# A two-layer decode block on one Trainium2 core: eight more units of K kept on the chip, a ring of 12 units, one narrow wo a layer, transposes for the gathers, and a last product in column fourths

## The chip, the core and the metric

The kernel runs on one core of one Trainium2 chip. The metric is device time in microseconds (us) of one execution; the time before the change is the median of three runs. The core has a matrix engine (PE, with its weight loads shown apart as PEld), a vector engine (DVE), a scalar engine (ACT), GpSimd (POOL) and a sync engine (SP), which here issues nearly all loads. Loads from the main memory (HBM) into the on-chip memory (SBUF) are carried by 16 DMA engines. PE writes to PSUM, which has eight banks of 128 partitions x 512 floats.

## The reference

Two equal layers, with the same weights and the same K and V caches. Two sequences (B = 2), one new token each, model width 512. Attention has 32 query heads of 128 and 8 KV heads; each KV head serves four query heads over 32768 cached positions. All is float32.

```python
def _A_ref(x, k_cache, v_cache, wq, wo):       # attention
    q = (x @ wq).reshape(B, Sq, Hq, Dh).transpose(0, 2, 1, 3)
    k, v = jnp.repeat(k_cache, rep, axis=1), jnp.repeat(v_cache, rep, axis=1)
    scores = jnp.einsum("bhqd,bhkd->bhqk", q, k) * (Dh ** -0.5)
    o = jnp.einsum("bhqk,bhkd->bhqd", _softmax(scores), v)
    return o.transpose(0, 2, 1, 3).reshape(B, Sq, Hq * Dh) @ wo
def _B_ref(x, w_gate, w_up, w_down):           # feedforward, 1792 wide
    return (_gelu(x @ w_gate) * (x @ w_up)) @ w_down

x = A_x
for layer in range(2):                          # the same weights and caches in both
    x = x + _A_ref(_layernorm(x), A_k_cache, A_v_cache, A_wq, A_wo)
    x = x + _B_ref(_layernorm(x), B_w_gate, B_w_up, B_w_down)
```

The two caches together have 2 x 268 MB. They don't fit on the chip, so each layer reads them anew.

## The kernel before

**Units and places.** SBUF is one array M of 110 units; a unit is 128 partitions x 512 floats, 256 KB. Three big slots A, B and C have 32 units each (0, 32 and 64 on), a zone from unit 96 has the rest; units 106 to 109 hold scratch. All loads stand in one list (`plan`), written out by hand in the order in which they are issued. `pump` (L105) issues the head of the list on SP as soon as its units are marked free, and never passes it; `free` (L120) marks units free where the program text has used them. So SP waits, in order, for the use of what stood in a place before.

**Attention.** A pair is one KV head g and one sequence b, 16 pairs a layer; layer 0 goes through them upward, layer 1 downward. K and V of a pair come in two halves each: four chunks (k0, k1, v0, v1) of 32 units, 8 MB, which pass through the three slots in turn. `scores` (L287) multiplies a 32-column window that holds the four queries with each unit of K (L282), into four column groups of a bank, and takes the maximum (`peak`). `softmax` (L299) exchanges the maxima, takes the exponentials on ACT and transposes them on PE (L310). `values` (L318) multiplies them with V (L326) into one bank. `combine` (L333) copies that bank to SBUF (L335), sums its pieces on PE with four products against a selection matrix (L337), and multiplies with the reciprocal sum (L339). After both sequences of a KV head, `project` (L341) multiplies by that head's part of wo, four units, into the bank W, where the residual x has been put beforehand (`restart`, L233).

**Center.** `center` (L238) copies W to SBUF with a row sum on ACT, and brings x and x minus its mean into columns on PE: eight instructions against a constant of four columns (L242) and a product of the row sums with -1/512 (L243); two copies take the results to xw (L245) and xin (L246). `deviation` makes 1/sqrt(variance).

**Feedforward.** `feedforward` (L348): the gate and up weights, 28 units (`gu`), are multiplied with xw (L363), first 16 units, then 12; `gelu` on ACT and DVE; `hidden` transposes the result (L392); `down` multiplies with the 14 units of `wd` (L407) into W. In layer 1 the last unit of wd goes another way: W is copied to SBUF (L422), the unit itself is the stationary operand of four products (L427), W's four groups are added with a selection matrix (L430), and a copy (L433) and a DMA (L434) give the output, 128 x 8 floats.

**The layer boundary.** The last pair of layer 0 is also the first of layer 1. Its v stays on the chip (64 units), of k1 the first 24 units stay (`KC1`), and of k0 five units are copied to PSUM banks (L466, L471): 93 units kept. The rest of the memory, 20 units, is a ring of five places of four units (`PL`, `RING`): through it come gu and wd of layer 0, wq of layer 1 (its last four units, `wq7`, first), then the eight missing units of k1 (L183 and L184). k0's other 27 units are loaded again (L185). The loop at L500 multiplies the seven query pieces and, after each, scores some of the k1 units that are kept, which frees their places for k0.

## Time and profile before

| what | value |
|---|---|
| median of three runs | 2578.67 us (2578.1 to 2579.88) |
| the profiled execution, its own time | 2578.3 us |
| span in it, first to last instruction | 2576.5 us |
| HBM read | 1105.03 MB, 429 GB/s over the span |
| PE busy; weight loads; DVE; ACT | 1373.9; 406.2; 130.8; 80.9 us |
| mean granted PE clock | 0.733 of full speed |
| instructions | 20195, of them 9430 matmuls and as many weight loads |

The profile is a page on one execution, taken by the hardware profiler, and answers that can be asked of its trace. A row of a group of instructions has the line, the engine and the operation, the tiles (written <- read), shapes and count, then the busy time, the mean of one in ns, and the engine's idle time before them with what ended it. `L326 PE` is line 326 on the matrix engine. A timeline row begins with the start and the duration in us, and ends with the idle time and its releaser in brackets. A row of the windows view begins with a stretch of time and has the busy time of each engine (with the count of instructions), the granted clock, the mean busy share of the 16 DMA engines, and GB/s. A row of DMA issues has the size and the median time from issue to landing. "SPq L114" is a DMA issue by SP. A float32 product is issued as two instructions, so four units are "x8"; a transpose is one.

### The profile page before, as it was taken

Reading aid. Unit: us, or ns where it says so; the run is one execution under the profiler, and the core shown is the slowest. Engines: PE = TensorE matmul, PEld = TensorE weight load, DVE = VectorE, ACT = ScalarE, POOL = GpSimd, SP = SyncE. Lnnn points to the kernel's source line nnn. Section 1 sums busy time; section 2 is a strip of 40 time slices with the busy share of each in tenths; the row PEclk is TensorE's granted clock in tenths of the full one; section 3 lists DMA queues with packets and bytes.
Section 4 is the critical chain, followed back from the end, with each engine's and each line's share of the span. In section 5 each row is a group of like instructions: output and inputs, shape, how many; then the busy total and the mean of one; then the engine's idle time right before and its main releaser. Section 6 shows DMA issues by size and latency. Waiting matters only on the chain.

```text
span 2576.5 us, 20195 instructions
## 1 busy us (share of the span) xinstructions
PE 1373.9 (53%) x9430; PEld 406.2 (16%) x9430; DVE 130.8 (5%) x390; ACT 80.9 (3%) x195; POOL 3.8 (0%) x12
## 2 busy tenths in 40 slices
PE   3554545455545544555576555454455544554556
PEld 1111111111111111111122111111111111111112
DVE  0000000000000000000010000000000000000001
ACT  0000000000000000000010000000000000000000
POOL 0000000000000000000000000000000000000000
PEclk9777777777766777777788677777767777776778
DMA  9999999999999999999999999999999999999998
GB/s 424 433 429 435 431 433 435 431 437 429 433 433 428 436 437 428 434 432 433 423 403 439 432 429 436 430 433 436 432 431 435 431 434 432 434 431 431 436 435 347
DMA packets 27587, 1106.33 MB, mean 429 GB/s; under 512 B 3312, under 2 KB 3440, under 8 KB 4208
## 3 DMA queue, kind: packets, MB, share of 16 engines
q1 hardware_dynamic: 27216, 1104.95, 99.5%
q8 instruction: 74, 1.21, 0.2%
q10 hardware_dynamic: 288, 0.09, 0.0%
q14 instruction: 9, 0.07, 0.0%
HBM read 1105.03 MB, written 0.00 MB: 429 GB/s over the span
## 4 chain that ended last, share of the span: by engine, by line
DMA 62%; PE 25%; another core or an unknown queue 12%; issue 0%; ACT 0%; DVE 0%; SPq 0%; DVEq 0%; ACTq 0%
DMA M<-in_vt 52%; PE bank L326 16%; DMA M<-in_kt 8%; PE bank L282 7%; DMA M<-in_wd 1%; PE bank L345 1%; PE bank L337 1%; DMA M<-in_gu 0%; DMA M<-in_wq 0%; ACT M L335 0%; PE bank L407 0%; PE bank L258 0%; PE bank L310 0%; DVE oT L339 0%
## 5 line engine op out<-in xcount | busy, mean ns | idle before, releaser
L282 PE MATMUL bank<-M,qw 128*32 128x512 f32 x4096 | 591.6, 741 | 544.9 <-DMA M<-in_kt 544.9
L326 PE MATMUL bank<-M 128*16 128x512 f32 x4096 | 580.3, 730 | 513.9 <-DMA M<-in_vt 513.9
L282 PEld LDWEIGHTS bank<-M,qw 128*32 128x32 f32 x4096 | 143.5, 133 | 981.0 <-DMA M<-in_kt 578.9
L326 PEld LDWEIGHTS bank<-M 128*16 128x16 f32 x4096 | 137.1, 112 | 930.4 <-issue 915.6
L285 DVE TENSOR_REDUCE sm<-bank 128x1 f32<-128x512 f32 x64 | 44.2, 691 | 1125.4 <-PE bank L282 1125.4
L307 ACT ACTIVATE M<-bank,sm 128x512 f32<-128x512 f32 x64 | 43.4, 683 | 1239.1 <-DVE sm L302 1239.1
L310 PE MATMUL bank<-cst,M 128*128 128x128 f32 x256 | 51.1, 348 | 42.2 <-ACT M L307 42.0
L339 DVE TENSOR_TENSOR oT<-bank,sm 128x4 f32<-128x4 f32 x32 | 5.2, 162 | 1138.8 <-PE bank L337 1138.8
L335 ACT COPY M<-bank 128x512 f32<-128x512 f32 x32 | 18.8, 586 | 1141.0 <-PE bank L326 1141.0
L311 DVE COPY M<-bank 128x512 f32<-128x512 f32 x64 | 43.8, 691 | 60.8 <-PE bank L310 60.8
L337 PE MATMUL bank<-cst,M 128*128 128x4 f32 x256 | 34.1, 256 | 22.5 <-ACT M L335 22.5
L310 PEld LDWEIGHTS bank<-cst,M 128*128 128x128 f32 x256 | 37.0, 176 | 52.5 <-ACT M L307 52.5
L337 PEld LDWEIGHTS bank<-cst,M 128*128 128x128 f32 x256 | 31.3, 192 | 52.0 <-ACT M L335 52.0
L301 PE MATMUL bank<-cst,sm 128*128 128x128 f32 x32 | 10.3, 323 | 35.1 <-DVE sm L300 35.1
L345 PE MATMUL bank<-M,oT 128*2 128x512 f32 x128 | 22.0, 765 | 4.1 <-DVE oT L339 4.1
L363 PE MATMUL bank<-M,xw 128*32 128x512 f32 x112 | 21.4, 737 | 4.6 <-DVE M L387 2.6
L315 PEld LDWEIGHTS bank<-cst,sm 128*128 128x128 f32 x128 | 23.1, 253 | 0.0
L315 PE MATMUL bank<-cst,sm 128*128 128x4 f32 x128 | 21.1, 270 | 0.0
L258 PE MATMUL bank<-M,xw 128*32 128x512 f32 x128 | 19.0, 706 | 2.1 <-DMA M<-in_wq 1.4
L235 PE MATMUL bank<-cst,xin 128*2 128x128 f32 x40 | 6.0, 301 | 23.3 <-DMA cst<-in_consts 23.3
L301 PEld LDWEIGHTS bank<-cst,sm 128*128 128x128 f32 x32 | 4.3, 133 | 64.1 <-DVE sm L300 64.1
L307 ACT ACTIVATION_READ_ACCUMULATOR M<-bank,sm 128x1 f32 x64 | 12.5, 196 | 0.0
(68 smaller groups left out, 128.5 us busy)
## 6 DMA issues: line engine op xcount, KB each, us to landing
M<-in_wo SPq DMA_DIRECT2D x16, 1024.0 KB, 51.1
M<-in_vt SPq DMA_DIRECT2D x6, 2048.0 KB, 43.0
M<-in_kt SPq DMA_DIRECT2D x3, 4096.0 KB, 18.0
M<-in_kt SPq DMA_DIRECT2D x5, 2048.0 KB, 15.5
M<-in_wq SPq DMA_DIRECT2D x2, 4096.0 KB, 17.0
M<-in_gu SPq DMA_DIRECT2D x8, 1024.0 KB, 23.4
M<-in_wq SPq DMA_DIRECT2D x8, 1024.0 KB, 9.3
M<-in_gu SPq DMA_DIRECT2D x3, 2048.0 KB, 33.2
```

The costliest lines, as they stand in the source:

```text
L258: nc.tensor.matmul(Q[32 * k:32 * k + 32, :], xw[:, k, XO - 2 * g:XO - 2 * g + 32], mem(u), start=start, stop=stop)
L282: nc.tensor.matmul(S[32 * t:32 * t + 32, :], w[:, 28 - 4 * c:60 - 4 * c], mem(u), start=start, stop=stop)
L285: nc.vector.tensor_reduce(mx[:, h:h + 1], S, axis=AX.X, op=OP.max)
L307: nc.scalar.activation(p[h], S[h], AF.Exp, bias=bias, scale=SCALE, accum_out=ls[:, h:h + 1])
L310: nc.tensor.transpose(S[h][:, k * P:(k + 1) * P], p[h][:, k * P:(k + 1) * P], ident)
L311: nc.vector.tensor_copy(mem(U_PT + h), S[h])
L315: nc.tensor.matmul(X[:, P:P + REP], ls[:, h:h + 1].to_broadcast([P, P]), mask, start=(h == 0), stop=(h == 1))
L326: nc.tensor.matmul(acc[32 * t:32 * t + 16, :], mem(U_PT + h)[:, k * P + 32 * t + 16 * e:k * P + 32 * t + 16 * e + 16], mem(u), start=(h == ...
L335: nc.scalar.copy(md, acc)
L337: nc.tensor.matmul(X[:, :REP], md[:, c * P:(c + 1) * P], sel[:, 4 * c:4 * c + 4], start=(c == 2), stop=(c == 1))
L345: nc.tensor.matmul(W[32 * t:32 * t + NB, :], oT[:, t, :], mem(u + t), start=(t > 0 and first), stop=final)
L363: nc.tensor.matmul(G[v][32 * t:32 * t + 32, :], xw[:, k, XO:XO + 32], mem(un), start=(k == 0), stop=(k == KC - 1))
```

## The change

- `KC1` goes: all 32 units of k1 stay, with 64 of v and five of k0 in PSUM, 101 units. The two loads of k1 go.
- The ring has three places of four units (`PL`). wq of layer 1 comes in pieces of 4 and 2 units, with places written out; `kseq` is the order in which k1 is scored, and the five units in PSUM are copied to places of k1 (`held`).
- `NARROW`: for KV head 6 in layer 0 and 1 in layer 1, query heads 2 and 3 of wo are loaded as before (two units), and heads 0 and 1 come as `wn`: the same 512 KB as 16 partitions x 16 units, written in the list after the last chunk of that KV head, into the slot whose turn it is. `project` multiplies them in 16 products of 16 rows, after it has brought oT into that form with eight small products and a copy. The slots of layer 1 follow from where layer 0 ends (`roles`).
- `combine` scales the copied bank with the reciprocal sum (`linvc`, made in `softmax`), transposes its four parts on PE and sums the pieces on DVE. `center` does likewise, and adds the mean's product on DVE.
- In layer 1's `down`, each unit of wd is multiplied in four parts of 128 columns, each into a column group of its own; `restart(split=True)` puts x there likewise. The output is the bank's first 128 columns as a whole, 128 x 128 floats, and the host picks rows from it.

```diff
@@ -33,18 +33,21 @@
-PL = [96, 100, 104, 88, 92]
+PL = [96, 100, 104]
-RING = [2, 3, 4, 0, 1]
-KC1 = 24
+RING = [2, 0, 1]
+NARROW = [6, 1]
+NH = 2
+NG = P // 16
+NC = NH * NG
...
@@ -111,7 +112,10 @@
-            nc.sync.dma_start(mem(u, n), src)
+            if key[0] == "wn":
+                nc.sync.dma_start(M[:16, u * U:(u + n) * U], src.rearrange("(e r) n -> e r n", r=4))
+            else:
+                nc.sync.dma_start(mem(u, n), src)
...
@@ -162,35 +166,49 @@
-            places.append(PL[RING[at % 5]])
+            places.append(PL[RING[at % 3]])
...
     def add_wo(l, g):
-        add(("wo", l, g), wo[g], PL[g % 2], 4)
+        if g == NARROW[l]:
+            add(("wo", l, g), cols(wo[g], NH, REP - NH), PL[g % 2], REP - NH)
+        else:
+            add(("wo", l, g), wo[g], PL[g % 2], REP)
+
+    def sequence(pairs, l):
+        todo = []
+        for n, (g, b) in enumerate(pairs):
+            todo += [(g, b, nm_, h) for nm_ in "kv" for h in range(2)]
+            if g == NARROW[l] and (n + 1 == len(pairs) or pairs[n + 1][0] != g):
+                todo.append((g, b, "w", 0))
+        return todo
     for l in range(2):
         if l == 0:
             stream("wq", 0, wq, 32, (16, 16), (SLOT_A, SLOT_A + 16))
             ring = [SLOT_B, SLOT_C, SLOT_A]
-            todo = [(g, b, nm_, h) for g, b in orders[0] for nm_ in "kv" for h in range(2)]
+            todo = sequence(orders[0], 0)
+            roles = [ring[(len(todo) - 4 + i) % 3] for i in range(3)]
         else:
-            ring = [SLOT_A, SLOT_B, SLOT_C]
+            last0, last1, lastv = roles
+            ring = [lastv, last0, last1]
             g, b = orders[1][0]
-            add(("wq7",), cols(wq, 28, 4), PL[RING[1]], 4)
-            ring_stream("wq", 1, wq, 28, 2)
-            add(("k1", 0), cols(kt[b, g, 1], KC1, 4), PL[1], 4)
-            add(("k1", 1), cols(kt[b, g, 1], KC1 + 4, 4), PL[2], 4)
-            stream("k0", 1, kt[b, g, 0], KFREE, (8, 8, 8, 3), [SLOT_C, SLOT_C + 8, SLOT_C + 16, PL[3]])
+            add(("wq7",), cols(wq, 28, 4), ZONE + 2, 4)
+            stream("wq", 1, wq, 28, (4, 2, 2, 4, 4, 2, 2, 4, 4), [ZONE + i for i in (6, 10, 0, 2, 6, 10, 0, 2, 6)])
+            stream("k0", 1, kt[b, g, 0], KFREE, (8, 8, 8, 3), [last1 + i for i in (0, 8, 16, 24)])
             g, b = orders[1][1]
-            chunk("k", 1, g, b, 0, SLOT_C, (8, 8, 16))
-            chunk("k", 1, g, b, 1, SLOT_A, (16, 16))
-            chunk("v", 1, g, b, 0, SLOT_B)
+            chunk("k", 1, g, b, 0, last1, (8, 8, 16))
+            chunk("k", 1, g, b, 1, lastv, (16, 16))
+            chunk("v", 1, g, b, 0, last0)
             add_wo(1, g)
-            chunk("v", 1, g, b, 1, SLOT_C)
-            todo = [(g, b, nm_, h) for g, b in orders[1][2:] for nm_ in "kv" for h in range(2)]
+            chunk("v", 1, g, b, 1, last1)
+            todo = sequence(orders[1][2:], 1)
         for i, (g, b, nm_, h) in enumerate(todo):
+            if nm_ == "w":
+                add(("wn", l, g), wn[l], ring[i % 3], NC)
+                continue
             last = i == len(todo) - 1
             second = (g, b) == orders[l][orders[l].index((g, b))] and orders[l].index((g, b)) % 2 == 1
             if nm_ == "v" and h == 1 and second and not last:
@@ -202,8 +220,8 @@
             ring_stream("gu", 0, gu, 28, 0)
             ring_stream("wd", 0, wd, 14, 7)
         else:
-            stream("gu", 1, gu, 28, (8, 8, 8, 4), [SLOT_C + 8 * i for i in range(4)])
-            stream("wd", 1, wd, 14, (4, 4, 2, 2, 1, 1), [SLOT_A + i for i in (0, 4, 8, 10, 12, 13)])
+            stream("gu", 1, gu, 28, (8, 8, 8, 4), [ring[(len(todo) - 3) % 3] + 8 * i for i in range(4)])
+            stream("wd", 1, wd, 14, (4, 4, 2, 2, 1, 1), [ring[(len(todo) - 2) % 3] + i for i in (0, 4, 8, 10, 12, 13)])
...
@@ -230,7 +247,11 @@
-    def restart(alone=False):
+    def restart(alone=False, split=False):
+        if split:
+            for c in range(KC):
+                nc.tensor.matmul(W[32 * c:32 * c + NB, :P], xin[:, c, :], ident, start=True, stop=False)
+            return
         for c in range(KC):
             nc.tensor.matmul(W[0:NB, c * P:(c + 1) * P], xin[:, c, :], ident, start=(c == 0),
                              stop=alone and c == KC - 1)
@@ -238,12 +259,11 @@
     def center():
         ws = mem(U_PT + 1)
         nc.scalar.activation(ws, W, AF.Copy, accum_out=rs)
-        for c in (2, 3, 0, 1):
-            nc.tensor.matmul(X[:, c * 4:(c + 1) * 4], ws[:, c * P:(c + 1) * P], two, start=(c == 2), stop=False)
-        nc.tensor.matmul(X[:, :KC * 4], rs.to_broadcast([P, P]), neg, start=False, stop=True)
-        xc = X[:, :KC * 4].rearrange("p (c w b) -> p c w b", w=2, b=NB)
-        nc.vector.tensor_copy(xw[:, :, XO:XO + NB], xc[:, :, 1, :])
-        nc.scalar.copy(xin, xc[:, :, 0, :])
+        for c in range(KC):
+            nc.tensor.transpose(X[:, c * P:(c + 1) * P], ws[:, c * P:(c + 1) * P], ident)
+        nc.tensor.matmul(A[:, :NB], rs.to_broadcast([P, P]), neg, start=True, stop=True)
+        nc.vector.tensor_reduce(xin, X.rearrange("p (c t r) -> p c r t", c=KC, t=4)[:, :, :NB, :], axis=AX.X, op=OP.add)
+        nc.vector.tensor_tensor(xw[:, :, XO:XO + NB], xin, A[:, :NB].unsqueeze(1).to_broadcast([P, KC, NB]), op=OP.add)
@@ -314,6 +334,7 @@
         for h in range(2):
             nc.tensor.matmul(X[:, P:P + REP], ls[:, h:h + 1].to_broadcast([P, P]), mask, start=(h == 0), stop=(h == 1))
         nc.vector.reciprocal(linv, X[:, P:P + REP])
+        nc.vector.tensor_tensor_reduce(junk, linv, mask, 1.0, 0.0, OP.mult, OP.add, linvc)
@@ -332,18 +353,34 @@
     def combine(acc, oT, g, b):
         md = mem(U_PT)
-        nc.scalar.copy(md, acc)
-        for c in (2, 3, 0, 1):
-            nc.tensor.matmul(X[:, :REP], md[:, c * P:(c + 1) * P], sel[:, 4 * c:4 * c + 4],
-                             start=(c == 2), stop=(c == 1))
-        nc.vector.tensor_tensor(oT[:, :, b], X[:, :REP], linv, op=OP.mult)
+        nc.scalar.activation(md, acc, AF.Copy, scale=linvc)
+        for c in range(4):
+            nc.tensor.transpose(X[:, c * P:(c + 1) * P], md[:, c * P:(c + 1) * P], ident)
+        full = X[:, :]
+        own = bass.AP(full.tensor, full.offset, [list(full.ap[0]), [1, REP], [P + REP, 4], [32, 4]])
+        nc.vector.tensor_reduce(oT[:, :, b], own, axis=AX.XY, op=OP.add)
     def project(l, g, oT):
         first, final = g == orders[l][0][0], g == orders[l][-1][0]
         u = at(("wo", l, g))
-        for t in range(REP):
-            nc.tensor.matmul(W[32 * t:32 * t + NB, :], oT[:, t, :], mem(u + t), start=(t > 0 and first), stop=final)
-        free(u, REP)
+        lo = NH if g == NARROW[l] else 0
+        for t in range(lo, REP):
+            nc.tensor.matmul(W[32 * t:32 * t + NB, :], oT[:, t, :], mem(u + t - lo), start=(t > 0 and first),
+                             stop=final)
+        free(u, REP - lo)
+        if lo:
+            u = at(("wn", l, g))
+            for i in range(NG):
+                nc.tensor.matmul(X[:16, 4 * i:4 * i + 4], ident[:, 16 * i:16 * i + 16], oT[:, :NH, :],
+                                 start=True, stop=True)
+            on = hT[:16].rearrange("p v j r -> p (v j r)")
+            nc.vector.tensor_copy(on, X[:16, :4 * NG])
+            for j in range(NC):
+                r, i = divmod(j, NG)
+                t = j % 4
+                nc.tensor.matmul(W[32 * t:32 * t + NB, :], on[:, 4 * i + 2 * r:4 * i + 2 * r + NB],
+                                 M[:16, (u + j) * U:(u + j + 1) * U], start=False, stop=False)
+            free(u, NC)
     def feedforward(l):
...
@@ -401,36 +438,30 @@
         def down(lo, hi):
-            for n in range(lo, min(hi, FD - tail)):
+            for n in range(lo, hi):
                 key, un = below[n]
                 at(key)
-                nc.tensor.matmul(W[32 * (n % 4):32 * (n % 4) + NB, :], part(n), mem(un),
-                                 start=(0 < n < 4), stop=(n + 4 >= FD - tail))
+                if final:
+                    for c in range(KC):
+                        nc.tensor.matmul(W[32 * c:32 * c + NB, :P], part(n), mem(un)[:, c * P:(c + 1) * P],
+                                         start=False, stop=(n == FD - 1))
+                else:
+                    nc.tensor.matmul(W[32 * (n % 4):32 * (n % 4) + NB, :], part(n), mem(un),
+                                     start=(0 < n < 4), stop=(n + 4 >= FD))
                 free(un)
-        restart()
+        restart(split=final)
-        if tail:
-            ws = mem(U_PT + 1)
-            nc.scalar.copy(ws, W)
-            for n in range(FD - tail, FD):
-                key, un = below[n]
-                at(key)
-                    nc.tensor.matmul(X[:, c * NB:(c + 1) * NB], mem(un)[:, c * P:(c + 1) * P], part(n),
-                                     start=(n == FD - tail and c == 0), stop=False)
-            for c in (2, 3, 0, 1):
-                nc.tensor.matmul(X[:, c * NB:(c + 1) * NB], ws[:, c * P:(c + 1) * P], sel[:, :NB],
-                                 start=False, stop=(c == 1))
-            y = sm[:, 0:8]
-            nc.vector.tensor_copy(y, X[:, :KC * NB])
+        if final:
+            y = mem(U_PT + 1)[:, :P]
+            nc.vector.tensor_copy(y, W[:, :P])
             nc.sync.dma_start(out, y)
...
@@ -495,39 +525,42 @@
     k1 = pieces[("k", 0, g, b, 1)]
     where = pieces[("wq", 1)]
     S0, S1, A1 = bank[0], bank[5], bank[1]
-    i, s = 0, 0
-    early = [0, 4, 4, 4, 4, 4, KC1]
+    kseq = list(range(16)) + [28, 29, 30, 31, 27] + list(range(16, 27))
+    ends = {i % 4: i for i in kseq}
+    todo, s = deque(kseq), 0
+    early = [0, 4, 4, 4, 4, 4, CH]
+    C0 = roles[1] + KFREE
+    held = {30: C0 + 1, 31: C0 + 2, 27: C0 + 3, 28: C0 + 4, 29: C0}
+
+    def store(i, on_act):
+        take(held[i], 1)
+        (nc.scalar.copy if on_act else nc.vector.tensor_copy)(mem(held[i]), bank[psum[i]])
+
     for m in range(7):
-        u = at(where[s][0])
         for j in range(4):
-            query_unit(X, m, j, u + j, m == 0, m == 6)
-        s += 4
-        free(u, 4)
+            key, u = where[s]
+            at(key)
+            query_unit(X, m, j, u, m == 0, m == 6)
+            s += 1
+        for j in range(4):
+            free(where[s - 4 + j][1])
         if m == 0:
             query_gather(mem(U_PT), Q7, 7, 1)
             w = window(g, b)
-        for j in range(min(early[m], KC1 - i)):
-            score_unit(S1, w, i, k1[i][1], i < 4, i >= CH - 4)
+        for j in range(min(early[m], len(todo))):
+            i = todo.popleft()
+            score_unit(S1, w, i, k1[i][1], i < 4, i == ends[i % 4])
             free(k1[i][1])
-            i += 1
-        if m == 4:
-            take(PL[3] + 3, 1)
-            nc.vector.tensor_copy(mem(PL[3] + 3), bank[psum[30]])
         if m == 5:
-            for q, kk in enumerate((31, 27, 28, 29)):
-                (nc.vector.tensor_copy if q % 2 else nc.scalar.copy)(mem(PL[4] + q), bank[psum[kk]])
+            for n, i in enumerate((30, 31, 27, 28)):
+                store(i, n % 2 == 0)
+    store(29, False)
     restart()
     query_copy(X, mem(U_PT + 1))
     query_gather(mem(U_PT + 1), X, 0, 7)
     wnext = window(*orders[1][1])
     where = pieces[("k0", 1)]
     peak(S1, 1)
-    held = {30: PL[3] + 3, 31: PL[4], 27: PL[4] + 1, 28: PL[4] + 2, 29: PL[4] + 3}
     seq = list(range(24)) + [30, 31, 27, 28, 29] + [24, 25, 26]
     left = {i % 4: i for i in seq}
     seen = set()
...
@@ -584,14 +617,16 @@
+        "wn": f(np.asarray(A_wo).reshape(HKV, REP, NG, 16, DM)[NARROW, :NH].transpose(0, 3, 1, 2, 4)
+                ).reshape(2, 16, NC * DM),
-    args.append(nc.dram_tensor("out", (P, KC, NB), F32, kind="ExternalOutput").ap())
+    args.append(nc.dram_tensor("out", (P, P), F32, kind="ExternalOutput").ap())
-    return f(got.transpose(2, 1, 0)).reshape(NB, 1, DM)
+    return f(np.asarray(got).reshape(KC, 32, P)[:, :NB].transpose(1, 0, 2)).reshape(NB, 1, DM)
```

More of the change, by code (lines that the diff above doesn't have):

```diff
@@ L39 @@
 XO = 14
-C_ID, C_SEL, C_SELT, C_TWO, C_NEG, C_MASK, C_PEN, C_PAR = 0, 128, 144, 152, 156, 160, 164, 168
-C_ALL = 170
+C_ID, C_SEL, C_SELT, C_NEG, C_MASK, C_PEN, C_PAR = 0, 128, 144, 152, 154, 158, 162
+C_ALL = 164
 NPS = 5
 KFREE = CH - NPS
-RING = [2, 3, 4, 0, 1]
-KC1 = 24
+RING = [2, 0, 1]
[3 more added lines that the diff above has]
+NC = NH * NG
 def constants():
@@ L60, in constants @@
     for b in range(NB):
-        c[r % 32 == b, C_NEG + NB + b] = -1.0 / DM
-        c[r % 32 == b, C_TWO + b] = 1.0
-        c[r % 32 == b, C_TWO + NB + b] = 1.0
+        c[r % 32 == b, C_NEG + b] = -1.0 / DM
     for b in range(NB):
@@ L72, in block_kernel @@
 @with_exitstack
-def block_kernel(ctx: ExitStack, tc: tile.TileContext, x, consts, kt, vt, wq, wo, gu, wd, out):
+def block_kernel(ctx: ExitStack, tc: tile.TileContext, x, consts, kt, vt, wq, wo, wn, gu, wd, out):
     nc = tc.nc
@@ L91, in block_kernel @@
     linv, sq2, rs, rstd2 = sm[:, 6:10], sm[:, 10:12], sm[:, 12:13], sm[:, 13:15]
-    rstd, junk, nscale, half, ones, var = (sm[:, 15:16], sm[:, 16:20], sm[:, 20:21], sm[:, 21:22], sm[:, 22:23],
-                                           sm[:, 24:26])
+    rstd, junk, nscale, half, ones, linvc, var = (sm[:, 15:16], sm[:, 16:20], sm[:, 20:21], sm[:, 21:22],
+                                                  sm[:, 22:23], sm[:, 23:24], sm[:, 24:26])
     def mem(u, n=1):
@@ L214, in block_kernel @@
     selt = cst[:, C_SELT:C_SELT + 8]
-    neg = cst[:, C_NEG:C_NEG + 4].unsqueeze(1).to_broadcast([P, KC, 4])
-    two = cst[:, C_TWO:C_TWO + 4]
+    neg = cst[:, C_NEG:C_NEG + NB]
     mask = cst[:, C_MASK:C_MASK + REP]
@@ L395, in feedforward @@
         below = pieces[("wd", l)]
-        tail = 1 if l == 1 else 0
+        final = l == 1
         def part(n):
@@ L462, in block_kernel @@
             k0 = pieces[("k", 0, g, b, 0)]
-            free(SLOT_C + KC1, CH - KC1)
             free(k0[0][1], KFREE)
@@ L524, in block_kernel @@
     where = pieces[("k0", 1)]
-    for i in range(KC1, CH):
-        u = at(("k1", (i - KC1) // 4)) + (i - KC1) % 4
-        score_unit(S1, w, i, u, False, i >= CH - 4)
-        free(u)
     peak(S1, 1)
-    held = {30: PL[3] + 3, 31: PL[4], 27: PL[4] + 1, 28: PL[4] + 2, 29: PL[4] + 3}
     seq = list(range(24)) + [30, 31, 27, 28, 29] + [24, 25, 26]
```

4 lines of the change are left out of this document (1 added, 3 removed).

## The prediction

> **What bounds the kernel now.** I read the page first, parts 2 to 4, then the windows view by stage, then the timeline of the two places where the windows view shows the DMA engines below full share.
>
> ```profile
> DMA  9999999999999999999999999999999999999998
> ...
> q1 hardware_dynamic: 27216, 1104.95, 99.5%
> q8 instruction: 74, 1.21, 0.2%
> ...
> DMA 62%; PE 25%; another core or an unknown queue 12%; issue 0%; ACT 0%; DVE 0%; SPq 0%; DVEq 0%; ACTq 0%
> ```
>
> The load queue q1 occupies 16 engines for 99.5% of the span, so every byte that is not loaded is time, as long as the queue stays full. The windows view shows where it does not:
>
> ```profile
> 64.00:1236.00 1172.00, 612.89 (x4207) 178.95 (x4203) 52.67 (x149) 31.61 (x77) 0.00 (x0) 0.72 1.00 432
> 1236.00:1287.00 51.00, 28.59 (x213) 7.63 (x209) 3.85 (x9) 2.62 (x6) 0.00 (x0) 0.80 0.98 418
> 1287.00:1292.00 5.00, 3.65 (x24) 1.07 (x16) 0.16 (x1) 0.91 (x2) 0.00 (x0) 0.76 0.90 374
> 1292.00:1301.00 9.00, 8.32 (x44) 3.74 (x44) 0.84 (x8) 0.53 (x3) 0.69 (x1) 0.57 0.86 319
> 1301.00:1318.00 17.00, 12.42 (x72) 3.26 (x68) 4.57 (x14) 3.26 (x8) 0.31 (x1) 0.90 1.01 413
> ...
> 1357.00:2520.00 1163.00, 611.39 (x4248) 177.81 (x4240) 55.95 (x156) 31.96 (x79) 0.00 (x0) 0.73 1.00 433
> ...
> 2563.00:2566.00 3.00, 2.74 (x26) 1.69 (x26) 0.47 (x2) 0.47 (x1) 0.30 (x1) 1.00 0.55 227
> 2566.00:2569.00 3.00, 1.97 (x18) 0.31 (x10) 1.76 (x6) 0.89 (x2) 0.01 (x1) 1.00 0.53 209
> 2569.00:2572.00 3.00, 2.73 (x14) 0.59 (x13) 0.17 (x1) 0.00 (x0) 0.00 (x0) 1.00 0.15 52
> ```
>
> The columns after the times are the busy times of PE, weight load, DVE, ACT and POOL, then granted clock, DMA share and GB/s. In both attention stages the share is 1.00 and PE is busy 613 of 1172 us, so what PE gains there is worth nothing. From 2563 to 2569 the share is 0.55 and 0.53: half of the engines have finished and the others work on for 6 us. Each load is dealt evenly over the engines, so half of them have fallen some 6 us behind. I put that down to the 74 instruction fetches of q8, which fall on single engines. A load has landed when its last engine is done, so the late half sets the time. At 1287 to 1301 the early half waits (share 0.90 and 0.86), which levels the engines at the layer's end.
>
> **Units not loaded.** All of the last chunk k1 is kept now, so two loads of 4 units, 1024 KB each, go away. The timeline has them between two PE starts that each ended a wait for a landing:
>
> ```profile
> 1335.19 1.07 PE L258 MATMUL bank<-M,xw 128*32 128x512 f32 x8 [0.56 <-DMA M<-in_wq]
> ...
> 1340.16 1.06 PE L282 MATMUL bank<-M,qw 128*32 128x512 f32 x8 [0.20 <-DMA M<-in_kt]
> 1345.15 3.64 PE L282 MATMUL bank<-M,qw 128*32 128x512 f32 x16 [3.92 <-DMA M<-in_kt]
> 1349.95 3.64 PE L282 MATMUL bank<-M,qw 128*32 128x512 f32 x16 [1.16 <-DMA M<-in_kt]
> ```
>
> Last wq piece to second k1 piece: 4.97 us for 8 units, 0.62 us a unit; the 8-unit pieces of k0 behind them, 4.8 to 5.0 us apart, agree. PE then scores 12 units of k1 after the last wq piece instead of 8; at 3.64 us for 8 units it still ends before the third k0 piece is due. So **-5.0 us**, all of it if the k0 loads are issued in time: their places are freed by early scores of k1 some 5 us before they are needed.
>
> **The narrow wo.** In each layer one wo loads 2 units less in the usual way, 1.24 us less on every engine, and the same 512 KB come as 16 rows of 16 units on 16 partitions, written as four outer rows of four. No load of before has this form. If it runs on four engines, each carries 8 units' worth, 4.95 us, or 3.7 us more than before on balance; if it is dealt over sixteen, nothing changes. Where the four are in the early half, they have 6 us to spare near the end of a layer, where both narrow loads stand (g = 6 and g = 1), and the late half gains 1.24 us in each layer. Where they are in the late half, each layer loses 3.7 us. The windows rows give no engine its number. [...] I take **-2.5 us**, with +7.4 and 0 as the other ends. [...]
>
> The 16-unit place of this load stands in the rotation of the three big slots. PE's extra products for it lie under the idle half of PE in the attention rows above. The load is queued on SP ahead of the next pair's k; it waits there for the scores of its own pair, which are long done:
>
> ```profile
> M<-in_kt SPq DMA_DIRECT2D x60, 50.5
> ```
>
> A chunk lands 50.5 us after its issue and takes 20, so 30 us of loads are ahead of it; one rotation shortened by some 15 us leaves cover. Without it, the next pair would start late by the difference; I cost it at 0.
>
> **The ring of 12 units.** The feedforward and query weights of the layer boundary pass through three places of 4 units instead of five. The timeline there:
>
> ```profile
> 1286.66 1.05 PE L326 MATMUL bank<-M 128*16 128x512 f32 x8 [1.44 <-DMA M<-in_vt]
> 1288.42 1.05 PE L337 MATMUL bank<-cst,M 128*128 128x4 f32 x8 [0.70 <-ACT M L335]
> 1292.42 1.87 PE L242 MATMUL bank<-cst,M 128*128 128x4 f32 x8 [0.81 <-ACT M L240]
> 1294.15 0.59 PE L243 MATMUL bank<-cst,sm 128*128 128x16 f32 x2
> 1294.78 0.17 DVE L245 COPY xw<-bank 128x8 f32<-128x8 f32 x1 [5.10 <-PE bank L243]
> 1295.00 1.94 PE L363 MATMUL bank<-M,xw 128*32 128x512 f32 x8 [0.26 <-DVE xw L245]
> 1301.61 1.88 PE L363 MATMUL bank<-M,xw 128*32 128x512 f32 x8 [0.27 <-DMA M<-in_gu]
> ...
> out<-sm SPq DMA_DIRECT2D x1, 4.0 KB, 1.4
> ```
>
> The last v landed at 1286.66. Behind it come wo and the gu pieces, 2.48 us each; six of them make 1301.5, just when PE starts on the fifth gu piece (1301.61), so the late engines never stop now. In the new ring gu0 and gu1 have free places, gu2 waits for the projection (in time), and gu3 waits until gu0 has been used. Now that is at 1296.94. The chain before it gets shorter: the sums of combine (1.05 us) become four transposes,
>
> ```profile
> 1260.03 1.33 PE L310 MATMUL bank<-cst,M 128*128 128x128 f32 x8 [1.31 <-ACT M L307]
> ```
>
> eight of which took 1.33 us, so 0.66; center's sums (1292.42 to 1294.74, 2.3 us) become four transposes and one product, 0.66 to 1.3 at the clock of 0.57 and some 0.45, with a second DVE step of 0.2. I take 1.0 us off in all (0 to 1.5): gu0 used at 1295.9. A load of almost nothing lands 1.4 us after its issue (the output's row), so gu3 can land 1.4 + 2.48 after 1295.9; in a full queue it would land 2.48 after gu2's 1296.6. Stall: 1295.9 + 1.4 - 1296.6 = **+0.7 us**. From then on a refill comes in time when its place is used within 4.95 - 1.4 = 3.5 us of landing. Four units took 1.04 to 1.94 us on PE. The tightest is the query load wq3, which waits for center:
>
> ```profile
> 1317.46 0.60 ACT L240 ACTIVATE M<-bank 128x512 f32<-128x512 f32 x1 [6.69 <-PE bank L407]
> 1319.75 1.47 PE L258 MATMUL bank<-M,xw 128*32 128x512 f32 x8 [0.26 <-DVE xw L245]
> ```
>
> From the last wd product to the first wq use done are 3.8 us; with 1.4 and some 1.5 for that product itself this is 6.7 us after the last wd landing, against 12 units (wq7, wq0, wq1, wq2) that the queue still has then, 7.4 us. So 0.7 in the sum, 0 to 3 as bounds.
>
> **The end.** The last unit of wd, its reduction and the output:
>
> ```profile
> 2571.06 0.09 PEld L407 LDWEIGHTS bank<-M,hT 128*2 128x2 f32 x2 [0.63 <-DMA M<-in_wd]
> 2572.01 1.05 PE L427 MATMUL bank<-hT,M 128*128 128x2 f32 x8
> 2572.16 0.59 ACT L422 COPY M<-bank 128x512 f32<-128x512 f32 x1 [4.96 <-PE bank L407]
> 2572.92 1.03 PE L430 MATMUL bank<-cst,M 128*128 128x2 f32 x8
> 2574.22 0.35 SPq L434 DMA_DIRECT2D out<-sm  x1
> ...
> 2565.76 1.04 PE L407 MATMUL bank<-M,hT 128*2 128x512 f32 x8 [0.26 <-DVE hT L393]
> L311 DVE COPY M<-bank 128x512 f32<-128x512 f32 x64 | 43.8, 691 | 60.8 <-PE bank L310 60.8
> ```
>
> Unit 12 was there at 2571.06, so 13 lands 0.62 later, at 2571.7; the output is issued 2.5 us after that. Now each unit is multiplied in four fourths of 128 columns that go to four different column groups. Four units in four groups took 1.04 us together, so one unit in fourths takes 0.26 to 1.04 (one behind another); I take 0.4. The copy of 128 columns lies between 0.17 and the 0.69 of 512; I take 0.3. With 0.1 for hand-overs the issue is 0.8 us after the landing, 1.7 earlier. The output has 64 KB instead of 4: a quarter unit, +0.15. Sum **-1.55**, bounds -0.9 and -1.8.
>
> **At no cost.** The extra DVE product behind the reciprocal, the scaled copy of combine, the smaller constants and the transposes of all other pairs lie beside loads at a share of 1.00; in the worst case the next loads have the 50 us lead above. The five copies from PSUM go to other places in the same stretch.
>
> **Sum.** The profiled execution took 2578.3 us (span 2576.5 and 1.8 around it): 2578.3 - 5.0 - 2.5 + 0.7 - 1.55 = 2569.95. The median shown is 2578.67, 0.4 more: **2570.4**.
>
> **Rivals.** *The four engines are late ones.* Then each layer's late half gets 3.7 us more instead of 1.24 less: 2570.4 + 2 x 4.95 = 2580.3. [...] The same time comes out if sixteen engines must share the 16 partitions' inlet. *The narrow load is dealt evenly:* 2572.9. *The ring gives the saved bytes back:* if center and combine gain nothing and the wq refills lose 1 us in a few rounds, the boundary loses 4 to 5 us: 2575. For: PE has a clock of 0.57 there. *The ring runs dry, slower than before:* 19 refills wait for a freed place. If use takes over 3.5 us from the landing, each is late; at 1 us each this is 19 us: 2570.4 - 0.7 + 19 = 2588.7. It decides from 0.5 us a refill on (2579). Against: 1.04 to 1.94 us a piece.
>
> **How the numbers follow.** Chances: the forecast 0.66, late engines 0.13, dealt evenly 0.09, saving given back 0.07, ring dry 0.05. The forecast's own range by its bounds is 2569.4 (no stall, end -1.8) to 2573.4 (stall 3, end -0.9); the low end of the range is 1.4 under it, 0.6 for the runs' own spread (2578.1 against 2578.67) and 0.8 for layer ends that level better than I reckon. Its high end, 2576, takes in the even deal and the given-back saving and leaves out the late engines and the dry ring, 0.18. A measurement here can tell 0.2%, 5.2 us: faster means under 2573.5. That is the forecast nearly whole and two thirds of the even deal, 0.70; late engines, given back and the rest are within it, 0.24; the dry ring is slower, 0.06.
>
> **What would show it.** Right: 1103 MB on q1; the k0 waits some 5 us nearer to the last wq; a share near 1.0 up to within 3 us of the last landing instead of 0.55 for 6 us; the output's issue under 1 us after the last wd landing; one dip of under 1 us of lost landing time at gu3. Wrong: a longer stretch at half share at the end, with few engines at work (late engines); waits for in_gu, in_wd and in_wq of 1 us and more in every round (dry ring); or a last copy that starts over 1.5 us after the landing.

## The result, and the profile after

After the change: 2592.53 us median of four runs (2591.15 to 2594.41), against 2578.67; ratio 1.0053, 95% interval 1.0041 to 1.0066. Slower, where faster was forecast, and 16.5 us above the range's high end. The profiled execution took 2591.15 us, 12.85 more than that of before. The page of after, the rows that answer to those shown of before:

```profile
DMA  9999999999999999999999999999999999999998
GB/s 422 436 435 428 431 435 434 430 436 435 429 429 436 436 433 428 435 391 433 415 359 429 440 432 432 432 436 431 433 433 432 434 431 433 433 433 415 411 435 365
...
q1 hardware_dynamic: 27280, 1102.92, 99.4%
...
DMA 61%; PE 26%; another core or an unknown queue 12%; issue 1%; ACT 0%; DVE 0%; SPq 0%; DVEq 0%; ACTq 0%
```

The bytes fell as forecast, and the share of busy time says that nothing is wrong: q1 is still on for 99.4% of the span. The row of GB/s says otherwise: slice 18 has 391, slice 21 has 359, slices 37 and 38 have 415 and 411, where 430 is usual. The share counts an engine as busy while a packet is on its way, however slowly: the next rows have a share of 1.01 at 437 GB/s and at 284. So read the bytes beside the share. The windows view finds two of the dips; its last two columns are DMA share and GB/s. Before, in the time of after's first narrow load, 1118 to 1136:

```profile
1118.00:1136.00 18.00, 5.81 (x28) 1.29 (x32) 0.00 (x0) 0.00 (x0) 0.00 (x0) 0.62 1.01 437
```

After, there and at the second narrow load:

```profile
1118.00:1136.00 18.00, 3.96 (x24) 0.99 (x28) 0.00 (x0) 0.00 (x0) 0.00 (x0) 0.62 1.01 284
...
2382.00:2400.00 18.00, 1.15 (x16) 0.18 (x8) 0.00 (x0) 0.00 (x0) 0.00 (x0) 0.66 1.02 306
```

Same share, a third of the rate gone. 18 us at 284 instead of 437 is 6.3 us of loads. The timeline of after shows the same loss at the next landmarks:

```profile
1292.78 1.05 PE L347 MATMUL bank<-M 128*16 128x512 f32 x8 [1.43 <-DMA M<-in_vt]
...
1305.11 1.54 PE L400 MATMUL bank<-M,xw 128*32 128x512 f32 x8 [1.40 <-DMA M<-in_gu]
1308.37 6.30 PE L400 MATMUL bank<-M,xw 128*32 128x512 f32 x23 [1.72 <-DMA M<-in_gu]
...
1317.07 1.04 PE L449 MATMUL bank<-M,hT 128*2 128x512 f32 x8 [1.41 <-DMA M<-in_wd]
1320.72 1.89 PE L449 MATMUL bank<-M,hT 128*2 128x512 f32 x8 [2.61 <-DMA M<-in_wd]
...
1364.23 5.03 PE L302 MATMUL bank<-M,qw 128*32 128x512 f32 x32 [2.09 <-DMA M<-in_kt]
...
2585.76 0.40 PE L446 MATMUL bank<-M,hT 128*2 128x128 f32 x8 [0.39 <-DMA M<-in_wd]
2586.23 0.29 DVE L464 COPY M<-bank 128x128 f32<-128x128 f32 x1 [2.20 <-PE bank L446]
2586.58 0.35 SPq L465 DMA_DIRECT2D out<-M  x1
```

and of before, the start that answers to 1364.23 (the others are in the prediction):

```profile
1354.85 5.12 PE L282 MATMUL bank<-M,qw 128*32 128x512 f32 x32 [1.26 <-DMA M<-in_kt]
```

Four stretches make the account. *To the last v of layer 0:* 1286.66 became 1292.78, +6.1. *From there to the third piece of k0:* 68.19 became 71.45, +3.3 although 4.97 us of loads are gone, so the ring lost 8.2. *From there to the last wd landing:* 1216.9 (with the prediction's 2571.7) became 1221.5, +4.7. *From that landing to the output's issue:* 2.5 became 0.8, -1.7, and the output lands 0.13 later. Sum +12.5; the span grew by 12.6.

### The profile page after: what moved, and what is told of

Its sections match the earlier page's. It is cut to its first block, busy times and chain, and to the rows that moved or that the text cites. A ratio compares the mean times of both kernels' runs of the same rounds, so it can differ in the third digit from the quotient of the medians.

```text
span 2589.1 us, 20230 instructions
## 1 busy us (share of the span) xinstructions
PE 1363.3 (53%) x9444; PEld 387.4 (15%) x9444; DVE 139.5 (5%) x460; ACT 82.9 (3%) x190; POOL 3.8 (0%) x12
## 3 DMA queue, kind: packets, MB, share of 16 engines
q1 hardware_dynamic: 27280, 1102.92, 99.4%
q8 instruction: 74, 1.21, 0.2%
## 4 chain that ended last, share of the span: by engine, by line
DMA 61%; PE 26%; another core or an unknown queue 12%; issue 1%; ACT 0%; DVE 0%; SPq 0%; DVEq 0%; ACTq 0%
DMA M<-in_vt 47%; PE bank L347 15%; DMA M<-in_kt 11%; PE bank L302 8%; DMA M<-in_gu 3%; DMA M<-in_wd 1%; PE bank L368 0%; PE bank L330 0%; PE bank L278 0%; ACT M L356 0%; PE bank L358 0%; DMA M<-in_wq 0%; PE bank L400 0%; PE bank L381 0%
## 5 line engine op out<-in xcount | busy, mean ns | idle before, releaser
L327 ACT ACTIVATE M<-bank,sm 128x512 f32<-128x512 f32 x64 | 43.4, 682 | 1233.8 <-DVE sm L322 1233.8
L330 PE MATMUL bank<-cst,M 128*128 128x128 f32 x256 | 50.5, 344 | 42.2 <-ACT M L327 42.0
L361 DVE TENSOR_REDUCE oT<-bank 128x4 f32<-128x64 f32 x32 | 7.2, 224 | 1131.7 <-PE bank L358 1131.7
L356 ACT ACTIVATE M<-bank,sm 128x512 f32<-128x512 f32 x32 | 22.0, 687 | 1150.1 <-PE bank L347 1150.1
L330 PEld LDWEIGHTS bank<-cst,M 128*128 128x128 f32 x256 | 36.3, 174 | 52.8 <-ACT M L327 52.8
L358 PE MATMUL bank<-cst,M 128*128 128x128 f32 x128 | 21.0, 287 | 25.8 <-ACT M L356 25.8
L358 PEld LDWEIGHTS bank<-cst,M 128*128 128x128 f32 x128 | 13.4, 141 | 55.3 <-ACT M L356 55.3
L368 PE MATMUL bank<-M,oT 128*2 128x512 f32 x120 | 16.6, 592 | 5.1 <-DVE oT L361 5.1
L327 ACT ACTIVATION_READ_ACCUMULATOR M<-bank,sm 128x1 f32 x64 | 12.5, 196 | 0.0
## 6 DMA issues: line engine op xcount, KB each, us to landing
M<-in_kt SPq DMA_DIRECT2D x3, 4096.0 KB, 16.5
```

Source lines behind the costliest of these rows:

```text
L327: nc.scalar.activation(p[h], S[h], AF.Exp, bias=bias, scale=SCALE, accum_out=ls[:, h:h + 1])
L330: nc.tensor.transpose(S[h][:, k * P:(k + 1) * P], p[h][:, k * P:(k + 1) * P], ident)
L356: nc.scalar.activation(md, acc, AF.Copy, scale=linvc)
L358: nc.tensor.transpose(X[:, c * P:(c + 1) * P], md[:, c * P:(c + 1) * P], ident)
L368: nc.tensor.matmul(W[32 * t:32 * t + NB, :], oT[:, t, :], mem(u + t - lo), start=(t > 0 and first), stop=final)
```

## The experiments

The theory: the narrow load takes 11 us because few partitions are written by many engines, and the ring takes 8 because its places are used late. The rivals are in the expectations.

**The parts one by one.** Without the narrow load:

```diff
-NARROW = [6, 1]
+NARROW = [8, 8]          # no such g: every wo is loaded whole
```

> All of wo is loaded in the usual form, the rest as changed. By the landings, the last v of layer 0 came 6.1 us later than before although nothing else ahead of it differs, and layer 1 from k0's end to the last wd took 4.7 us more. Theory 1 (the narrow load is what costs there): 2592.5 - 10.8 = 2581.7 us. Rival (the ring of 12 units and what follows from it is the whole loss, the narrow load is free): 2592 us. If the ring costs what the landings at the layer boundary say (8.2 us), what is left over before is 8.2 - 5.0 - 1.4 = 1.8 us, that is 2580.5.

Measured: 2579.65 us, before on that chip 2578.28, ratio 1.0005 (0.9996 to 1.0015). The last v lands at 1286.6, as before. The two narrow loads cost 12.9 us together, and what is left of the change comes out as no change.

The kernel before with the new sums and the column fourths only (`combine`, `center`, `restart`, `feedforward` of after; ring and loads of before):

> The kernel before with the transposes in combine and center and the column fourths at the end, nothing else: 93 units kept, ring of 20 units, wo whole. Theory (only the end is on the path, 1.5 us): 2578.67 - 1.5 = 2577.2. Rival (the shorter sums also shorten the layer boundary): 2576.2. Rival (nothing of it is on the path): 2578.7.

Measured: 2577.06 us, ratio 0.9994 (0.9985 to 1.0004), about -1.2, which is not clear of the noise. So the ring of twelve, which saves 4.97 us, lost in the run without the narrow load 2579.65 - 2578.28 + 4.97 + 1.2 = 7.5 us by the medians, some 2.4 us to each side by the ratio's interval. In that run's profiled execution, 1.2 us longer than the median, the stretch from the last v to the third piece of k0 shows 9.3.

**Which engines, and what is crowded.** Single packets of after: each narrow load went as 16 packets of 32 KB, one on each of 16 engines, not on four: none of them starts where another ends. They took 1.7 to 4.0 us, where such a row took 1.21 us in the strided run below, and 64 KB packets beside them up to 6.5 us instead of 2.42. Four loads in place of one, each of every fourth partition:

```diff
-nc.sync.dma_start(M[:16, u * U:(u + n) * U], src.rearrange("(e r) n -> e r n", r=4))
+for r in range(4):
+    nc.sync.dma_start(M[r:16:4, u * U:(u + n) * U], src[r:16:4])
```

> As changed, but the narrow load is issued as four loads of four rows each (rows r, r+4, r+8, r+12), so that it can run on no more than four engines. Against the kernel without the narrow load (about 2581.7): theory 1 with four engines of the early half: 1.24 us less in each layer, 2579.3; with four of the late half: 3.7 us more in each, 2589. Rival (the cost comes from the slot that it takes in the rotation, or from the long rows, whichever engines carry it): 2592 as changed.

And one load to every seventh partition, `M[0:106:7, ...] <- src`:

> As changed, but the 16 rows of the narrow load go to partitions 0, 7, 14 ... 105 instead of 0 to 15, still as one load of 16 rows of 16 units; the products read partitions 0 to 15, so the two query heads' part of wo is left out of the result. Theory 1 (sixteen engines crowd into the inlet of 16 neighbouring partitions): the cost is gone, 2582 (1 more or less). Rival (long rows, one a engine, or the slot's shortened rotation): 2592 as changed.

Measured: 2607.27 us (ratio 1.0111, 1.0096 to 1.0127) and 2614.18 us (1.0136, 1.0119 to 1.0152). The times test something else, which the timeline of the first shows:

```profile
1129.82 0.29 DVE L323 CUSTOM_DVE_ANT_1 M<-bank,cst 128x128 f32<-128x128 f32 x1 [30.79 <-DMA M<-in_wn]
...
1142.52 0.34 SPq L119 DMA_DIRECT2D M<-in_kt  x1
```

The softmax's write to its scratch units, which the load does not touch, waited 30.79 us for the load. In after, where the load writes neighbouring partitions, the same write waited 0.53 us, for PE. What makes a strided target different was not tried by itself. The next k went out at 1142.5 instead of 1116.8, and the queue ran empty: 0 GB/s from 1128.7 to 1139.8. The packets still tell: in the first, sixteen rows on four engines at 1.21 us each and nothing beside them slow; in the second, rows of 1.9 to 2.2 us as long as other loads ran, then 1.21, and 64 KB packets beside them of up to 3.9 us. So sixteen partitions far apart lessened the crowding and did not end it.

Four loads of four neighbours each (`M[4*e:4*e+4] <- src[4*e:4*e+4]`), which brings no such wait:

> The changed kernel with its narrow load cut into four loads of four neighbouring partitions each, M[0:4], M[4:8], M[8:12], M[12:16]: no strided destination, so no wait of the softmax for it as in the two runs before. In the run with four strided loads the sixteen 32 KB rows ran four after another on four engines at 1.21-1.22 us each and no 64 KB packet beside them took more than 2.43 us. Theory (the 12.9 us that the narrow loads cost come from sixteen engines that write to sixteen neighbouring partitions at once): four engines, rows of 1.21 us, none of the neighbours slow, and the load ends with the early engines, so each layer is left with the -1.24 us of its bytes: 2579.65 - 2.5 = 2577.2 us. Rival one (four engines, but they are late ones at the landing): up to +3.7 us a layer, 2587 us. Rival two (a destination of sixteen partitions is slow, whatever writes to it): 2592 us, as the changed kernel.

The same 512 KB on 64 partitions, and on 128:

```diff
+nc.sync.dma_start(M[:64, u * U:(u + 4) * U], src.rearrange("e (c n) -> (e c) n", c=4))     # 64
+nc.sync.dma_start(M[:, u * U:(u + 2) * U], src.rearrange("e (c n) -> (e c) n", c=8))       # 128
```

> The changed kernel with the same 512 KB of each narrow load written as four units on each of 64 neighbouring partitions, in one load over sixteen engines. It leaves out three quarters of the narrow rows' part of two heads: project reads four of the sixteen units four times over, so the result is not the reference's. Theory (crowding on sixteen partitions): packets are at most a little over 1.21 us for 32 KB, neighbours stay at 2.42 us, 2579.65 - 2.5 = 2577 us, with up to +2 for what is left of the crowding on half of the partitions. Rival (the form of the load, its rows or its place in the queue, is what costs): 2592 us.

> The changed kernel with the same 512 KB, which lie side by side in memory, written as two units on each of all 128 partitions, in one load over sixteen engines. It leaves out seven eighths of the narrow rows' part of two heads: project reads two of the sixteen units eight times over, so the result is not the reference's. Two theories are left after the runs before, since four engines and 64 partitions were slow as well, and every engine slowed, not only those with a narrow row. Destination theory (the load crowds the partitions that it writes to): on all 128 partitions the crowding is gone, every packet goes at its usual pace, 2577.2 us. Source theory (the sixteen rows lie in 512 KB of memory, and engines that read so close together at one time stop each other and everybody behind them): as slow as before, 2590 us or a little under.

Sixteen partitions, the load's form and its place in the queue as in after, with the source's rows 512 KB apart in memory in place of side by side:

> [...] Source theory: rows of 1.21 to 1.3 us, neighbours at 2.42 us, 2579.65 - 2.5 = 2577.2 us, to 2578 if the load's first byte is late. Destination theory: rows of 1.7 to 4 us and slow neighbours as in the changed kernel, 2592 us.

Measured: blocks 2584.7 us, ratio 1.002 (1.0011 to 1.003); 64 partitions 2590.07, 1.0047 (1.0034 to 1.006); 128 partitions 2581.47, 1.0005 (0.9996 to 1.0014); far source 2593.04, 1.0055 (1.0043 to 1.0068). The same window of these four, in this order:

```profile
1118.00:1136.00 18.00, 2.78 (x20) 0.69 (x20) 0.00 (x0) 0.00 (x0) 0.00 (x0) 0.57 1.02 324
```
```profile
1118.00:1136.00 18.00, 3.47 (x24) 0.89 (x28) 0.00 (x0) 0.00 (x0) 0.00 (x0) 0.62 0.99 324
```
```profile
1118.00:1136.00 18.00, 7.03 (x48) 1.74 (x52) 0.00 (x0) 0.00 (x0) 0.00 (x0) 0.62 1.00 431
```
```profile
1118.00:1136.00 18.00, 2.56 (x16) 0.60 (x20) 0.00 (x0) 0.00 (x0) 0.00 (x0) 0.61 1.00 288
```

Moving the source's rows apart changed nothing; where the load writes does. But 64 partitions were nearly as bad as 16, and four engines crowded as well, which "few partitions" did not say. The blocks' time alone would also fit four late engines (rival one). The packets say otherwise for the first narrow load: at 1125.9 us four narrow rows were under way, and beside them twelve 64 KB packets, each of which took 3.5 to 4.8 us. At the second the blocks kept 419 GB/s from 2382 to 2400, where after had 306; why they crowded there so little is open. My expectations of 2577.2 also took off 2.5 us that a load over sixteen engines cannot save, since it brings the bytes that it replaces; for 128 partitions 2579.65 is the right figure, and the interval of its ratio, 2577.8 to 2582.5 us, holds it.

So the loads were measured by themselves, six of 512 KB in a row in each form:

> Leaves out the whole computation: it only loads, and its output is zeros. After three 64 KB x 128 loads it loads the same 512 KB six times in a row, in seven forms one after another, each form ended by a wait for all of it: two units on 128 partitions, four on 64, eight on 32, sixteen on 16, sixteen on 16 in four loads of neighbouring partitions, in four loads of every fourth partition, and sixteen on partitions 0, 8, 16 to 120. Then each form once more, once, between two loads of 64 KB x 128. Theory (what is short is the inlet of the partitions written to, as the narrow rows showed): six loads on 128 partitions take 3.1 MB / 430 GB/s = 7.3 us, on 64 partitions twice that, on 32 four times, on 16 some eight times; on every eighth partition 7.3 us; between two big loads the same forms slow their neighbours. Rival (each form runs at full pace by itself, and slows only beside packets that go to all partitions): 7.3 us for every form that uses sixteen engines alone, 64 KB packets over 3 us only in the last seven groups. For four strided loads against four blocks: by the theory both four engines at 1.21 us a row as in the strided run, 6 x 4.85 = 29 us; by the rival too.

The windows of the seven forms, in the order of the expectation (columns: time, DVE, POOL, PE clock, DMA share, GB/s):

```profile
62.80:72.80 10.00, 0.00 (x0) 0.00 (x0) 1.00 0.87 313
74.90:90.30 15.40, 0.00 (x0) 0.00 (x0) 1.00 0.99 203
92.50:107.90 15.40, 0.00 (x0) 0.00 (x0) 1.00 0.98 204
110.20:138.50 28.30, 0.00 (x0) 0.00 (x0) 1.00 0.98 110
141.20:184.70 43.50, 0.00 (x0) 0.00 (x0) 1.00 0.24 72
187.20:217.20 30.00, 0.00 (x0) 0.00 (x0) 1.00 0.25 105
219.40:234.50 15.10, 0.00 (x0) 0.00 (x0) 1.00 0.95 198
```

The rates come in halves, not by the number of partitions, as the theory had it: 64 and 32 alike, and sixteen partitions eight apart as fast as 32 neighbours. The four-engine loads of blocks made 72 GB/s, the strided ones 105 with the same number of engines (share 0.24 and 0.25). Six of the seven fit one map, my inference from these rates: an inlet, by estimate some 27 GB/s (110 / 4), serves four neighbouring partitions and the four that lie 32 further in the same half of 64; sixteen inlets in all. The seventh, the blocks, lies by the same estimate between four engines in one inlet at a time, 27, and in four inlets, 110, so the map alone does not give it.

The second half of the same run has each form between two loads of 64 KB x 128. The three loads together, with the form on 128, 64 and 16 partitions, and in blocks:

```profile
236.70:277.90 41.20, 0.00 (x0) 0.00 (x0) 1.00 0.99 420
279.70:322.40 42.70, 0.00 (x0) 0.00 (x0) 1.00 0.99 405
...
368.80:414.30 45.50, 0.00 (x0) 0.00 (x0) 1.00 0.99 380
416.00:472.40 56.40, 0.00 (x0) 0.00 (x0) 1.00 0.89 307
```

The neighbours slow there too: single 64 KB packets took up to 4.9 us beside the 16 partitions and 8.1 beside the blocks. But 64 partitions cost 1.5 us more than 128 here, and in the kernel 4.3 us for each load; that difference stays open.

The map was put to seven places that it tells apart, and inside the kernel:

> Leaves out the whole computation: it only loads, and its output is zeros; the same form as the run of loads alone, with other places. Theory (a map read from the seven rates of that run: four neighbouring partitions share an inlet of some 27 GB/s, and with them the four that lie 32 further on in the same half of 64, so there are sixteen inlets of eight partitions): six loads of 512 KB run at the pace of the inlets that they reach. 64 partitions from 0: 8 inlets, 207 GB/s. 64 partitions from 32: 16 inlets, full pace, some 310 to 430 GB/s with the start. 64 partitions from 64: 207. Sixteen rows on every fourth partition from 0 to 60: 207. On every fourth from 32 to 92: full pace, 310 to 430. On every second from 0 to 30: 207. On 56 to 71: 4 inlets, 107. Rival (what counts is how many partitions are written, or how far they spread): the three loads on 64 partitions alike at 207, the two on every fourth alike at 207.

> The changed kernel with each narrow load's 512 KB on partitions 32 to 95, four units on each, in place of partitions 0 to 63 (2590.1 us) or two units on all 128 (2581.5 us). It leaves out the narrow rows' part of two heads: project reads partitions 0 to 15, which this load does not write. Theory of the inlets: partitions 32 to 95 reach all sixteen, so it goes as on 128 partitions, 2581.5 us, up to 2584 if its rows meet those of neighbouring loads. Rival (the number of partitions counts): 2590 us.

```profile
63.00:78.60 15.60, 0.00 (x0) 0.00 (x0) 1.00 1.00 202
81.30:90.30 9.00, 0.00 (x0) 0.00 (x0) 1.00 0.90 350
92.30:108.10 15.80, 0.00 (x0) 0.00 (x0) 1.00 0.98 199
110.50:125.90 15.40, 0.00 (x0) 0.00 (x0) 1.00 0.97 202
128.50:137.60 9.10, 0.00 (x0) 0.00 (x0) 1.00 0.92 335
139.60:155.00 15.40, 0.00 (x0) 0.00 (x0) 1.00 0.98 204
157.20:185.50 28.30, 0.00 (x0) 0.00 (x0) 1.00 0.97 108
```

Seven of seven: 202, 350, 199, 202, 335, 204, 108 GB/s. 64 partitions from 32 on are fast, 64 from 0 on are not; between two big loads, too, they took 41.5 us in place of 42.8. In the kernel, the same form moved from partition 0 to 32:

```profile
1118.00:1136.00 18.00, 7.33 (x44) 1.69 (x44) 0.00 (x0) 0.00 (x0) 0.00 (x0) 0.62 1.00 431
```

and 2580.13 us, ratio 1.001 (1.0001 to 1.0019), against 2590.07: ten us for a start partition. The map gives thirteen of the fourteen rates, all but the blocks'. By it partitions 0 to 15 reach four inlets (110 GB/s alone). It does not say why packets beside a narrow load slow as well: in the blocks twelve neighbours were slow at one time, and the loads reach four inlets of sixteen; that stays open. The runs do show that the set of partitions alone doesn't decide. The same sixteen, filled by four engines, made 105 GB/s strided and 72 in blocks. By the map a strided load's four rows go to four inlets and a block's four rows to one; that this is the cause was not shown.

**The ring.** Without the narrow load, the ring of twelve cut into six places of two units:

```diff
-            cuts.append(min(4, total - n))
-            places.append(PL[RING[at % 3]])
+            cuts.append(2)
+            places.append(TWOS[at % 6])     # TWOS = [104, 106, 96, 98, 100, 102]
```

> The kernel without the narrow loads (2579.65 us), with the ring of twelve units cut into six places of two units in place of three of four, every load of the ring two units, and the query units given back one by one. Theory (the ring's loss of about 7.5 us comes from places that are used late: four units wait until the last of them has been used, at 0.9 us a unit with the clock at half and three column groups): half a place waits half as long, the loss falls to about 3 us, 2575 us. Rival (the loss is a fixed time from each issue to its first packet, some 1 us, on every refill): there are twice as many refills, the loss grows, 2580 to 2587 us.

And the kernel before with the new sums and four places of four units, 28 units of k1 kept:

> The kernel before with the new sums (2577.06 us) and a ring of four places of four units: 28 of the last k1's units kept, four loaded again, one wo in each layer whole. Saves 4 units, 2.48 us. Theory (the loss comes when three places in flight cover less than the time from a use to the next landing): with a fourth place another 5 us are in flight, the stalls of 0.7 to 2.65 us of the ring of twelve are gone but for the first, 2577.06 - 2.5 + 0.5 = 2575.1 us. Rival one (every place given up costs as much as the bytes it saves): 2577.1 us. Rival two (the late use stops the queue as in the ring of twelve): 2577.06 - 2.5 + 7.5 = 2582 us.

Measured: 2575.86 us, ratio 0.9987 (0.9979 to 0.9996), and 2575.39 us, 0.9988 (0.9979 to 0.9996). Both are faster than the kernel before by some 0.12%, intervals just clear of 1, and both are faster than the changed one. The loss in the ring, by the same sum as above: twos 2575.86 - 2578.41 + 4.97 + 1.2 = 3.6 us, sixteen units 2575.39 - 2577.06 + 2.48 = 0.8. Each is some 2 us to each side, so 3.6 and 0.8 are not told apart. In the run without the narrow load, gu3's issue and the first use of what it loaded:

```profile
1295.90 0.33 SPq L118 DMA_DIRECT2D M<-in_gu  x1
...
1300.71 1.06 PE L400 MATMUL bank<-M,xw 128*32 128x512 f32 x8 [2.70 <-DMA M<-in_gu]
```

It landed at 1300.67, 4.77 us after its issue, and the queue had run empty meanwhile; the first wd piece took 4.87 us there and 4.94 in after. The boundary in the same run, 35 us from the last v on:

```profile
1287.00:1322.00 35.00, 23.55 (x126) 7.58 (x120) 5.83 (x24) 4.10 (x9) 1.00 (x2) 0.72 0.83 310
1322.00:1357.00 35.00, 27.64 (x196) 9.38 (x192) 4.07 (x15) 2.93 (x6) 0.69 (x1) 0.89 1.00 394
```

in twos:

```profile
1287.00:1322.00 35.00, 27.31 (x150) 7.07 (x147) 6.69 (x31) 5.36 (x12) 1.54 (x3) 1.00 0.95 364
1322.00:1357.00 35.00, 28.07 (x206) 8.34 (x200) 3.43 (x9) 1.76 (x3) 0.15 (x1) 0.95 1.02 422
```

and with sixteen units:

```profile
1287.00:1322.00 35.00, 25.61 (x148) 7.61 (x144) 6.70 (x31) 5.31 (x12) 1.00 (x2) 0.80 0.96 378
1322.00:1357.00 35.00, 25.61 (x200) 7.72 (x196) 3.30 (x8) 1.72 (x4) 0.69 (x1) 0.90 1.01 424
```

The rate comes back with the smaller places though there are twice as many refills, so the loss is not a fixed time for each issue. The granted clock is 1.00 in twos and 0.72 in the run with three places; which of the two causes the other was not separated. Sixteen units in eight places of two:

> The kernel with a ring of sixteen (2575.39 us) with its places cut into eight of two units, each load of the ring two units and the query units given back one by one. Theory (late use of whole places): what is left of the ring's loss, some 0.8 us, falls to 0.3: 2574.9 us. Rival (twice as many refills, each with its issue): 2576 to 2578 us.

Measured: 2575.65 us, ratio 0.9988 (0.9979 to 0.9997): no further gain is seen, where 0.5 us was forecast, which these intervals can't show. With four places, what late use still costs is too little to see.

## Why the prediction was wrong, step by step

- **What bounds the kernel:** right. The bytes saved came out, and everything lost was lost in loads. But a full share was read as a full rate, which the rows at 1118 contradict.
- **Units not loaded, -5.0:** right, as far as the account can separate it. The ring of sixteen, which saves half, gained 1.7 us of its 2.48.
- **The narrow wo, -2.5:** the step that failed. It ran +6.1 and +4.7, 13.3 us off. "If it runs on four engines" was wrong: it ran on sixteen. No run shows what sets the number of engines, and none shows the term of -2.5: that four early engines carry the load was my assumption. In its place the runs showed sixteen packets of 32 KB on sixteen engines and 12.9 us for the two loads (2592.53 - 2579.65). The four strided loads of four partitions ran on four, 1.21 us a row. Then "if it is dealt over sixteen, nothing changes" was wrong too: I counted bytes for each engine, and not where they enter. My bounds, +7.4 and 0, came from counting bytes alone. The text named the inlet in half a sentence among the rivals and priced it with the late engines' 2580.3; by itself it takes the sum to 2569.95 + 13.3 = 2583.2.
- **Whether four early engines would have gained 1.24 us a layer** stays open. In the strided run four engines did it at full pace, 1.21 us a row, and ended beside the late half, but the wait that it brought hid the time. The late half at the end, which the forecast expected to shrink, stayed: a share of 0.67 and 0.51 from 2577 to 2583.
- **The ring, +0.7:** the second step that failed; it ran +8.2 in after and 7.5 without the narrow load. Two of its terms were too small. The first is the price of a use. I took "1.04 to 1.94 us a piece", the work of four units by itself. The rows of after at 1308.37 show 23 matmul rows in a row for 6.30 us: the second half of gu goes to three column groups, and the granted clock is 0.50 from 1308.4 to 1312, so the piece that landed at 1308.24 was used up at 1311.98, 3.7 us later. The second is the refill, "1.4 + 2.48" from issue to landing, 3.88 us, which also gave the condition of use within 3.5 us. Refills of four units into an emptied queue took 4.77 to 4.94 us, so the condition is a use within some 2.6 us of landing. In after the wd refill issued at 1311.99 would by 3.88 us have come 0.2 us late; it came 1.3 us late, and the next one as well: 1.41 and 2.61 us of PE idle. So the rival "the ring runs dry", given 0.05, was the right mechanism at 7.5 us instead of 18.3. How much of it each of the two terms makes was not separated.
- **The end, -1.55:** right: issue 0.82 us after the last landing, output 0.13 later. The copy took 0.29, the fourths 0.40, as taken.
- **Sum:** 2569.95 + 13.3 + 7.5 = 2590.75, for 2591.15 measured. That they agree confirms little: 13.3 and 7.5 are taken from the runs that they explain.
- **The cases:** two of the rivals came true together. I had priced each alone, so the highest time that had a chance was 2588.7.

## What to carry to other kernels

A load's place on the chip was a cost of its own here (324 GB/s with 64 partitions from 0 on, 431 from 32 on): try other partitions, count by rates like these the inlets that they reach, not only bytes and engines, and look for a full busy share beside a low rate in GB/s (1.01 beside 284). Price a ring by the time from a piece's landing to its last use in the stage's real order and clock, by what a refill takes from issue to landing when the queue has run empty (4.8 to 4.9 us for four units here), and by how many pieces are in flight meanwhile: here one place more gave up 2.5 us of saved bytes and got some 6.7 us of loss back, and places half as large got some 3.9 us back. When an edit has two risky steps, price them together too.

## What was not expected

- One load of 512 KB on 16 neighbouring partitions slowed all sixteen engines for some 15 us, those with ordinary 64 KB packets as well (up to 6.5 us for 2.42).
- Moving the same load from partitions 0 to 63 to partitions 32 to 95 brought 324 GB/s back to 431.
- A strided range of partitions as a load's target brought a wait of 30.79 us between things that share no byte.
